# Starting a chunked-attention and feed-forward kernel: units 0 and 1 prepared one after the other, q and k transposed on TensorE, and a new order in block 1

## The chip, the cores and the metric

The kernel runs on one core of a Trainium2 chip. The metric is the device time of one execution in microseconds. Before the change it is 287.82 us, the median of two runs (287.47 and 288.17).

The engines are named as in the profile: PE is the matrix engine (TensorE), with PEld for its loads of weights, DVE is VectorE, ACT is ScalarE, POOL is GpSimd and SP is SyncE. Each engine works through its own instructions in the order in which the program issues them.

## The reference

```python
def _attn_ref(q, k, v):                      # 8 x 8 x 576 x 64
    B, H, S, D = q.shape
    chunk = 64
    ...
    scores = scale * np.matmul(q_c, k_c.transpose(0, 1, 2, 4, 3))
    scores = scores - np.max(scores, axis=-1, keepdims=True)
    attn = np.exp(scores)
    attn = attn / (np.sum(attn, axis=-1, keepdims=True) + 1e-09)
    out = np.matmul(attn, v_c)
    return out.reshape(B, H, S, D).astype(np.float32)

def _moe_ref(x, w_in, w_out, beta):          # 4608 tokens, 512 -> 2048 -> 512
    h = x @ w_in
    g = h * (1.0 / (1.0 + np.exp(-beta * h)))
    return (g @ w_out).astype(np.float32)
```

The attention works inside chunks of 64 tokens of one head. Its output, with the heads side by side, is the input x of the two layers.

## The kernel before

The 4608 tokens are cut into 18 units of 256 tokens, and two units make one of 9 blocks of 512 tokens. For each unit the kernel makes the attention output, normalises it and transposes it, so that the model dimension lies on the partitions (`xt`, one per block). For each block, layer 1 (`emit_m`, L322) makes 16 pieces of 128 hidden features: four products with a slice of `w_in` into a PSUM bank `hps`, a tanh on ACT into `sg` (L339), and (tanh + 1) times h on DVE into `gt` (L343). With beta halved that is twice the gated value, and the 0.5 is put into the copy of the output. Layer 2 (`emit_t`, L354) makes four tiles of 128 tokens, 16 products each, into a bank `ops`; ACT copies it (L371) and SP stores it. Operands are float16, sums float32.

The attention of a unit is: q and k loaded by POOL's queue, which turns float32 into float16; transposed by DVE in blocks of 32 x 32 (`emit_T`, L145); scores (`emit_sc`, L216) as small products that use parts of the PE array side by side; the exponential on ACT (L247) into `et`; products with V (`emit_pv`, L254), in which a column of ones in V's tile gives the sum; a reciprocal and a multiplication on DVE (`emit_norm`, L280). The transpose of the result is either done on PE with a copy by ACT or DVE behind it (`emit_xt_pe`, L298, and `emit_xt_pair`, L306, for a whole unit), or by a transposing DMA of SP for later units.

PSUM has eight banks: four rotate under the tag "p" (`hps`, `ops`, idle products and others), two form the one buffer "s" and two the one buffer "x". A buffer is given out again only when everything that reads it has finished.

The order of all instructions is written out by hand (`tc.manual_schedule()`, L394). From block 3 on a list of due times merges the pieces (L563 to L596); the change touches nothing there.

The start, L395 to L467, handles units 0 and 1 together. SP loads q and k of heads 0 to 3 for both units as float32 (L399 to L404), 512 KB each; POOL loads heads 4 to 7 as float16. Each partition holds four neighbouring tokens, so unit 0 lies on partitions 0 to 63 and unit 1 on 64 to 127. POOL then loads four V tiles, sets `late` between them (L411), builds the identity, and loads the slices of `w_in`, of `w_out` and the next units. PE begins with 78 tiny products and idle products of 512 columns (`emit_idle`, L381), which only keep PE at work; one of them waits for `late` (L425). `emit_T_half(0)` (L174) casts heads 0 to 3 on ACT and transposes them on DVE, `emit_sc_half` (L186) makes scores of four heads of one unit, `emit_ex_half` (L206) their exponential. Then unit 0's products with V, unit 1's scores, normalisation and transposes follow, with idle products between them. Layer 1 begins at L452 with the first four pieces of unit 0's 256 columns (`emit_m(0, m, 0, 256)`), after them come the same four pieces for unit 1's columns (L464), then pieces 4 to 15 for all 512 columns.

Block 1's attention lies in layer 2 of block 0 (L469 to L489): 16 steps of four products, with unit 2's scores at step 8, its products with V at step 10, the transposed pair at step 13, unit 3's scores at step 14 with the exponential in two halves (`split`), and at step 15 the first piece of layer 1 of block 1, unit 3's products with V and its normalisation. The first five pieces of that layer are made for unit 2's columns first (L482 to L494), and the rest for all 512 columns (L495), with the missing halves between them (L498).

The softmax here doesn't subtract the row's maximum and nothing guards it: scores larger than these inputs give would overflow.

## Time and profile before

| What | Value |
|---|---|
| median of the two runs | 287.82 us |
| the profiled execution, its own time | 287.57 us |
| its span, from first to last instruction | 285.8 us |
| instructions | 6671 |
| first product of layer 1 | 15.16 us |
| first product of its second column half | 17.59 us |
| DVE busy, ACT busy, share of the span | 50%, 51% |
| bytes moved by DMA | 37.40 MB |

All times in the profile count from the start of the span. The profiled execution takes 1.8 us longer than its span. The profile gives, for each engine, the time in which it was busy and what ended the time in which it was not; the chain that ended last is followed back from the last instruction, and its share by engine says which engine sets the time. An engine that waits outside that chain costs nothing.

### The profile page before, as it was taken

Reading aid. Unit: us, or ns where it says so; the run is one execution under the profiler, and the core shown is the slowest. Engines: PE = TensorE matmul, PEld = TensorE weight load, DVE = VectorE, ACT = ScalarE, POOL = GpSimd, SP = SyncE. Lnnn points to the kernel's source line nnn. Section 1 sums busy time; section 2 is a strip of 40 time slices with the busy share of each in tenths; the row PEclk is TensorE's granted clock in tenths of the full one; section 3 lists DMA queues with packets and bytes.
Section 4 is the critical chain, followed back from the end, with each engine's and each line's share of the span. In section 5 each row is a group of like instructions: output and inputs, shape, how many; then the busy total and the mean of one; then the engine's idle time right before and its main releaser. Section 6 shows DMA issues by size and latency. Waiting matters only on the chain.

```text
span 285.8 us, 6671 instructions
## 1 busy us (share of the span) xinstructions
PE 279.2 (98%) x2779; PEld 136.5 (48%) x2779; DVE 143.6 (50%) x268; ACT 146.2 (51%) x223; POOL 95.6 (33%) x125
## 2 busy tenths in 40 slices
PE   6989999999999999999999999999999999999995
PEld 3564456544544444444444444444444444444444
DVE  2678444776558553535454536363635463333301
ACT  4478228773557545455554555554546444444411
POOL 8853678488073991168607000000000000000000
PEclk9999999999999999999999999999999999999999
DMA  8999999999999999999999983425311221010012
GB/s 198 177 197 206 182 179 213 209 164 150 207 104 173 178 176 162 170 190 187 168 170 164 174 130 78 100 57 119 79 54 39 73 57 55 37 39 37 37 73 76
DMA packets 141085, 37.40 MB, mean 131 GB/s; under 512 B 128000, under 2 KB 136576, under 8 KB 141056
## 3 DMA queue, kind: packets, MB, share of 16 engines
q0 software_dynamic: 99136, 17.83, 82.3%
q1 hardware_dynamic: 41776, 19.09, 32.5%
q8 instruction: 22, 0.36, 0.5%
q10 hardware_dynamic: 144, 0.07, 0.1%
q14 instruction: 7, 0.06, 0.0%
HBM read 36.71 MB, written 9.44 MB: 161 GB/s over the span
## 4 chain that ended last, share of the span: by engine, by line
PE 96%; POOL 1%; ACT 1%; issue 1%; DVE 0%; DVEq 0%; POOLq 0%
PE hps L329 44%; PE ops L361 43%; PE warm L381 2%; PE x L266 2%; PE sc L238 1%; PE ops L602 1%; PE sc L225 1%; PE y L266 1%; ACT xt L304 1%; POOL h L401 1%; PE sc L198 1%; POOL vbig L113 1%; PE xp L303 0%; ACT et L208 0%; PE xp L311 0%
## 5 line engine op out<-in xcount | busy, mean ns | idle before, releaser
L343 DVE SCALAR_TENSOR_TENSOR gt<-sg,hps 128x512 f16<-128x512 f32 (+1 forms) x153 | 99.2, 655 | 101.9 <-ACT sg L339 101.3
L329 PE MATMUL hps<-xt,win 128*128 128x512 f16 (+1 forms) x612 | 136.2, 367 | 0.8 <-ACT xt L304 0.7
L339 ACT ACTIVATE sg<-hps,beta 128x512 f32<-128x512 f32 (+1 forms) x153 | 100.4, 662 | 71.3 <-PE hps L329 69.7
L361 PE MATMUL ops<-wout,gt 128*128 128x512 f16 x560 | 131.1, 379 | 0.0
L329 PEld LDWEIGHTS <-win 128*128 128x128 f16 x612 | 58.3, 98 | 62.4 <-issue 1.0
L361 PEld LDWEIGHTS <-gt 128*128 128x128 f16 x560 | 54.1, 98 | 64.0
L371 ACT ACTIVATE osb<-ops 128x512 f32<-128x512 f32 x35 | 20.9, 598 | 42.8 <-PE ops L361 42.8
L113 POOL DMA_DIRECT2D vbig<-in_v_dram x40 | 34.0, 867 | 11.9 <-DMA wout<-in_moe_w_out_dram 3.6
L99 POOL DMA_DIRECT2D qu<-in_q_dram x22 | 18.7, 859 | 24.9 <-DMA qT<-qu 22.5
L287 DVE TENSOR_TENSOR x<-x,rd 128x512 f16<-128x512 f32 x27 | 18.7, 691 | 1.0
L99 POOL DMA_DIRECT2D ku<-in_k_dram x22 | 18.7, 874 | 0.9 <-DMA ku<-in_k_dram 0.9
L285 DVE RECIPROCAL rd<-x 128x8 f32<-128x8 f32 x27 | 5.4, 199 | 13.1 <-PE x L266 13.1
L247 ACT ACTIVATE et<-sc 128x1024 f16<-128x1024 f32 (+1 forms) x8 | 6.4, 811 | 8.7 <-PE sc L238 8.7
L231 ACT ACTIVATE et<-sc 128x1024 f16<-128x1024 f32 x10 | 10.2, 1021 | 0.7
L266 PEld LDWEIGHTS <-et 64*64 64x64 f16 x576 | 6.0, 107 | 7.4 <-issue 4.7
L381 PE MATMUL warm<-idle 128*128 128x512 f16 (+1 forms) x32 | 8.0, 401 | 0.0
L287 DVE TENSOR_TENSOR x<-y,rd 128x256 f16<-128x256 f32 x18 | 7.6, 424 | 0.6
L105 POOL DMA_DIRECT2D ku<-in_k_dram x9 | 6.8, 755 | 2.6 <-DMA win<-in_moe_w_in_dram 1.3
L105 POOL DMA_DIRECT2D qu<-in_q_dram x9 | 6.8, 766 | 1.5 <-DMA win<-in_moe_w_in_dram 0.7
L266 PE MATMUL x<-vbig,et 64*64 64x65 f16 x432 | 6.7, 194 | 0.2 <-ACT et L208 0.2
L614 DVE TENSOR_SCALAR osb<-ops 128x256 f32<-128x256 f32 (+1 forms) x2 | 0.7, 358 | 12.1 <-PE ops L602 12.1
L131 POOL DMA_DIRECT2D win<-in_moe_w_in_dram x8 | 6.0, 767 | 1.4 <-DMA vbig<-in_v_dram 1.4
(46 smaller groups left out, 75.3 us busy)
## 6 DMA issues: line engine op xcount, KB each, us to landing
out_dram<-osb SPq DMA_DIRECT2D x35, 256.0 KB, 3.6
vbig<-in_v_dram POOLq DMA_DIRECT2D x32, 128.0 KB, 7.8
qu<-in_q_dram POOLq DMA_DIRECT2D x20, 128.0 KB, 5.7
ku<-in_k_dram POOLq DMA_DIRECT2D x20, 128.0 KB, 7.4
win<-in_moe_w_in_dram POOLq DMA_DIRECT2D x8, 256.0 KB, 8.9
wout<-in_moe_w_out_dram POOLq DMA_DIRECT2D x4, 512.0 KB, 12.2
qu<-in_q_dram POOLq DMA_DIRECT2D x3, 256.0 KB, 7.4
ku<-in_k_dram POOLq DMA_DIRECT2D x3, 256.0 KB, 7.9
```

Of the source, the lines that this page charges most:

```text
L99: nc.gpsimd.dma_start(out=tv[off:off + n, sp], in_=src[b, :, s:s + n, :].rearrange("h p d -> p h d"),)
L105: nc.gpsimd.dma_start(out=t[off // 2:(off + n) // 2], in_=src[b, :, s:s + n, :].rearrange("h (p r) d -> p h r d", r=2),)
L113: nc.gpsimd.dma_start(out=vbig[off:off + n, i, :, 0:D], in_=v[b, :, s:s + n, :].rearrange("h p d -> p h d"),)
L231: nc.scalar.activation(out=et, in_=sc, func=ACTF.Exp, scale=scale)
L266: nc.tensor.matmul(out=(x[0][64 * c:64 * c + 64, r, g, 0:D + 1] if len(x) == 1 else x[r][64 * c:64 * c + 64, g, 0:D + 1]), lhsT=(et[64 * r ...
L287: nc.vector.tensor_tensor(out=o, in0=z[..., 0:D], in1=rd[:, r].to_broadcast(list(o.shape)), op=ALU.mult)
L329: nc.tensor.matmul(out=hps[:, 0:n], lhsT=w_in16[m // 2][:, kk, (m % 2) * 128:(m % 2) * 128 + 128], rhs=xr[:, c0 // CH:(c0 + n) // CH, 2 * ...
L339: nc.scalar.activation(out=sg[:, 0:n], in_=hps[:, 0:n], func=ACTF.Tanh, scale=beta2[:, m:m + 1])
L343: nc.vector.scalar_tensor_tensor(out=gt_t[j][:, m, c0:c0 + n], in0=sg[:, 0:n], scalar=1.0, in1=hps[:, 0:n], op0=ALU.add, op1=ALU.mult,)
L361: nc.tensor.matmul(out=ops, lhsT=gt_t[j][:, kk, t * 128:(t + 1) * 128], rhs=w_out16[kk // 4][:, kk % 4, :], start=(kk == 0), stop=(kk == K ...
L371: nc.scalar.activation(out=osb, in_=ops, func=ACTF.Copy, scale=0.5)
L381: nc.tensor.matmul(out=d[:, 0:w], lhsT=idle[:, 0:128], rhs=idle[:, 0:w])
```

## The change

At the start, units 0 and 1 are handled apart. The float32 loads on SP and on ACT's queue now bring q and k of unit 0 for all heads, heads 0 to 3 on partitions 0 to 63 and heads 4 to 7 on partitions 64 to 127, 256 KB per load; POOL loads those of unit 1 in the same layout, in four loads, behind the identity and two V tiles and ahead of the first slice of `w_in`. Instead of DVE's transposes, PE transposes q and k with the identity into PSUM, and ACT and DVE copy them into `qkT0`: for unit 0 in 16 transposes of 128 columns, for unit 1 in 32 of 64 columns. The casts of unit 0 are shared between ACT and DVE. The scores of a unit are then 32 products over 64 rows in place of 64 over 32 rows with two summands. Layer 1 begins with two pieces of unit 0 between unit 1's scores and its products with V. The tile `late` and the wait for it go; a tile `spare` is there for one early exponential and for eight small copies after block 0's layer 1.

In block 1, unit 2's scores, its products with V and its transposed pair stand at steps 10, 12 and 14 of layer 2; unit 3's scores come after the last step, with one exponential for all of them, then three pieces of layer 1, then unit 3's products with V. Seven pieces instead of five are made for unit 2's columns first.

```diff
-    late = const.tile([128, 16], FP16)
+    spare = const.tile([128, 1], FP16)
...
-    qkT0 = [[const.tile([128, HH, 128, 2], FP16, name=f"t0{i}{a}") for i in range(2)] for a in range(2)]
+    qkT0 = [[const.tile([128, 2, 2, 64, 4], FP16, name=f"t0{i}{u}") for i in range(2)] for u in range(2)]
...
-    def emit_T_half(a):
-        for i, h0, h1 in ((0, 0, HH), (1, 0, HH // 2), (1, HH // 2, HH)) if a == 0 else ((0, 0, HH), (1, 0, HH)):
-            src = qk0[a][i][:, h0:h1]
-            if a == 0:
-                nc.scalar.copy(out=src, in_=raw0[i][:, h0:h1])
...
-    def emit_sc_half(u, a):
...
+    tq_t = {}
+
+    def emit_cast_first(i, hp, cast):
+        hs = slice(2 * hp, 2 * hp + 2)
+        to = qk0[0][i].rearrange("p h r d -> p (h r d)").rearrange("p (r h d) -> p h r d", r=4, h=HH)
+        cast(out=to[:, hs], in_=raw0[i][:, hs])
+
+    def emit_T_first(u, i, hp):
+        if (u, i) not in tq_t:
+            tq_t[u, i] = ps_p.tile([128, 2, 4, 128], FP16, tag="p", name="tq")
+        z = qk0[u][i].rearrange("p h r d -> p (h r d)")
+        for r in range(4):
+            if u == 0:
+                nc.tensor.transpose(
+                    out=tq_t[u, i][:, hp, r, :],
+                    in_=z[:, (r * HH + 2 * hp) * D:(r * HH + 2 * hp + 2) * D], identity=ident)
+                continue
+            for hh in range(2):
+                o = ((2 * hp + hh) * 4 + r) * D
+                nc.tensor.transpose(
+                    out=tq_t[u, i][64 * hh:64 * hh + 64, hp, r, :], in_=z[:, o:o + D], identity=ident)
+
+    def emit_cp_first(u, i, hp, copy):
+        hp = hp if isinstance(hp, slice) else slice(hp, hp + 1)
+        copy(
+            out=qkT0[u][i][:, hp].rearrange("p g a i r -> p g (a i) r"),
+            in_=tq_t[u, i][:, hp].rearrange("p g r x -> p g x r"),
+        )
+
+    def emit_sc_first(u):
+        et_t[u] = et_p.tile([128, 2, H, CH], FP16, tag="et", name="et")
+        sc = x_t["sc", u] = ps_s.tile([128, 2, H, CH], FP32, tag="s", name="sc")
+        qt, kt = (z.rearrange("p g a i r -> p g a (i r)") for z in qkT0[u])
+        for s in range(2):
+            for a in range(2):
+                for hp in range(2):
+                    for par in range(2):
+                        for c in range(2):
+                            t0 = 128 * s + 64 * c
+                            nc.tensor.matmul(
+                                out=sc[64 * c:64 * c + 64, par, 4 * s + 2 * a + hp, :],
+                                lhsT=kt[64 * par:64 * par + 64, hp, a, t0:t0 + 64],
+                                rhs=qt[64 * par:64 * par + 64, hp, a, t0:t0 + 64],
+                            )
+
+    def emit_ex_first(u, s):
+        js = slice(4 * s, 4 * s + 4)
...
-    def emit_pv(u, where=("x", "s")):
-        et = et_t.pop(u)
-        for s in (1, 0) if u >= MU else (0, 1):
+    def emit_pv(u, where=("x", "s"), which=None):
+        et = et_t[u]
+        for s in which or ((1, 0) if u >= MU else (0, 1)):
...
-                            lhsT=(et[64 * r:64 * r + 64, s, 4 * c + g, :] if u < XU else
+                            lhsT=(et[64 * r:64 * r + 64, s, 4 * c + g, :] if 2 <= u < XU else
...
-    def emit_xt_pe(u, s, copy=nc.scalar.copy):
+    def emit_xt_pe(u, s, copy=nc.scalar.copy, tag=None):
...
-        tag = "s" if u < 2 and (u, s) != (1, 0) else "xp"[s]
+        tag = tag or "xs"[s]
...
-        for a, eng, dst in ((0, nc.sync, raw0), (1, nc.gpsimd, qk0[1])):
+        def load_first(u, engs, dst):
             for i, src in enumerate((q, k)):
-                eng.dma_start(
-                    out=dst[i],
-                    in_=src[0, HH * a:HH * a + HH, 0:2 * UNIT, :].rearrange("h (p r) d -> p h r d", r=4),
-                )
+                for a in range(2):
+                    engs[a].dma_start(
+                        out=dst[i][64 * a:64 * a + 64],
+                        in_=src[0, HH * a:HH * a + HH, u * UNIT:(u + 1) * UNIT, :].rearrange(
+                            "h (p r) d -> p h r d", r=4),
+                    )
+
+        load_first(0, (nc.sync, nc.scalar), raw0)
+        nc.scalar.activation(out=spare, in_=tiny[:, 0:1], func=ACTF.Exp)
+        make_identity(nc, ident)
         bv = moe_beta.rearrange("(m w f) -> w m f", w=4, f=32)
         for w in range(4):
             nc.sync.dma_start(out=braw[32 * w:32 * w + KFF, :], in_=bv[w])
-        for i in range(4):
-            load_v(i)
-            if i == 1:
-                nc.gpsimd.memset(late, 0.0)
+        load_v(0)
+        load_v(1)
+        load_first(1, (nc.gpsimd, nc.gpsimd), qk0[1])
+        load_w_in(0)
+        load_v(2)
+        load_v(3)
         nxt[0] = 2
-        make_identity(nc, ident)
-        for g in range(8):
+        for g in range(1, 8):
             load_w_in(g)
         for g in range(3):
             load_w_out(g)
@@ -419,83 +439,96 @@
         load_w_out(3)
...
-        emit_tiny(78)
+        emit_tiny(85)
         warm = idle_bank()
+        emit_idle(7, 512, warm)
+        act_cp, vec_cp = nc.scalar.copy, nc.vector.tensor_copy
+        for i in range(2):
+            emit_cast_first(i, 0, act_cp)
+            emit_cast_first(i, 1, vec_cp)
+            emit_T_first(0, i, 0)
+            emit_cp_first(0, i, 0, act_cp)
+            emit_T_first(0, i, 1)
+            emit_cp_first(0, i, 1, vec_cp)
+            emit_idle((3, 1)[i], 512, warm)
+        nc.vector.transpose(out=bt, in_=braw)
+        emit_sc_first(0)
+        emit_ex_first(0, 0)
+        emit_ex_first(0, 1)
         emit_idle(3, 512, warm)
-        nc.tensor.matmul(out=warm[:, 0:16], lhsT=idle[:, 0:128], rhs=late)
-        emit_idle(8, 512, warm)
-        emit_T_half(0)
-        emit_sc_half(0, 0)
-        emit_ex_half(0, 0)
+        emit_pv(0, "xs", (0,))
+        emit_norm(0, 0)
+        emit_idle(2, 512, warm)
+        emit_pv(0, "xs", (1,))
+        emit_norm(0, 1)
+        emit_T_first(1, 0, 0)
+        emit_T_first(1, 0, 1)
+        emit_cp_first(1, 0, slice(0, 2), act_cp)
         warm = idle_bank()
-        emit_idle(6, 512, warm)
-        emit_T_half(1)
-        nc.vector.transpose(out=bt, in_=braw)
-        emit_sc_half(0, 1)
-        emit_ex_half(0, 1)
-        emit_sc_half(1, 0)
+        emit_xt_pe(0, 0, tag="x")
+        emit_T_first(1, 1, 0)
+        emit_T_first(1, 1, 1)
+        emit_cp_first(1, 1, 0, act_cp)
         emit_idle(2, 512, warm)
+        emit_xt_pe(0, 1, vec_cp, tag="x")
+        emit_cp_first(1, 1, 1, vec_cp)
+        emit_idle(1, 512, warm)
+        emit_sc_first(1)
+        emit_ex_first(1, 0)
+        emit_ex_first(1, 1)
         loads_to(5)
-        emit_pv(0, ("s", "p"))
-        emit_sc_half(1, 1)
-        emit_ex_half(1, 0, 2)
-        emit_norm(0, 0)
-        emit_norm(0, 1)
+        nc.scalar.activation(out=beta2, in_=bt[:, 0:KFF], func=ACTF.Copy, scale=0.5)
+        d = [emit_m(0, m, 0, 256, True) for m in (0, 1)]
+        emit_pv(1, "xs", (0,))
+        emit_norm(1, 0)
         emit_idle(1, 512, warm)
-        emit_idle(12, 64, warm)
-        emit_xt_pe(0, 0)
-        emit_pv(1, ("x", "p"))
+        emit_idle(13, 64, warm)
+        emit_pv(1, "xs", (1,))
         emit_norm(1, 1)
-        emit_norm(1, 0)
-        nc.scalar.activation(out=beta2, in_=bt[:, 0:KFF], func=ACTF.Copy, scale=0.5)
-        emit_xt_pe(0, 1)
-        d = [emit_m(0, m, 0, 256, True) for m in (0, 1)]
         d[0][0]()
-        emit_xt_pe(1, 1)
+        d.append(emit_m(0, 2, 0, 256, True))
+        emit_xt_pe(1, 0, tag="x")
         d[1][0]()
-        d.append(emit_m(0, 2, 0, 256, True))
-        d[0][1]()
-        emit_xt_pe(1, 0, nc.vector.tensor_copy)
         d.append(emit_m(0, 3, 0, 256, True))
-        for act, _ in d[2:]:
-            act()
-        for _, vec in d[1:]:
+        emit_xt_pe(1, 1, tag="s")
+        d[2][0]()
+        d[3][0]()
+        for _, vec in d:
             vec()
         for m in range(4):
             emit_m(0, m, 256, 256)
         for m in range(4, KFF):
             emit_m(0, m)
         emit_T(2)
+        for _ in range(8):
+            nc.scalar.activation(out=spare, in_=tiny[:, 0:1], func=ACTF.Copy)
         for i in range(16):
-            if i == 8:
+            if i == 10:
                 emit_sc(2)
-            if i == 10:
+            if i == 12:
                 emit_pv(2)
                 emit_norm(2, 0)
                 emit_norm(2, 1)
                 emit_T(3)
-            if i == 13:
+            if i == 14:
                 emit_xt_pair(2)
-            if i == 14:
-                emit_sc(3, True)
-            if i == 15:
-                a0, v0 = emit_m(1, 0, 0, 256, True)
-                a0()
-                emit_pv(3)
-                emit_norm(3, 0)
-                emit_norm(3, 1)
-                v0()
-                emit_m(1, 1, 0, 256)
             emit_t(0, i % 4, 4 * (i // 4), 4 * (i // 4) + 4)
-        emit_xt_pe(3, 0)
-        emit_m(1, 2, 0, 256)
-        emit_xt_pe(3, 1)
+        emit_sc(3)
+        for m in range(3):
+            emit_m(1, m, 0, 256)
+        emit_pv(3)
+        emit_norm(3, 0)
+        emit_norm(3, 1)
         emit_m(1, 3, 0, 256)
         emit_m(1, 4, 0, 256)
-        for m in range(5, KFF):
+        emit_xt_pe(3, 0)
+        emit_m(1, 5, 0, 256)
+        emit_xt_pe(3, 1)
+        emit_m(1, 6, 0, 256)
+        for m in range(7, KFF):
             emit_m(1, m)
-            if m < 10:
-                emit_m(1, m - 5, 256, 256)
+            if m < 14:
```

The lines that the diff cuts out of `emit_T_half`, `emit_sc_half` and `emit_ex_half` are removed as a whole; `emit_ex_first(u, s)` is the exponential of four of the eight columns of heads of one unit. With `tag` not given, `emit_xt_pe` takes the buffer "x" for a unit's first tile and "s" for the second; before, it took "x" and a bank of "p" for units above 1. That touches units 3 and 5, whose calls stand at L490, L492, L525 and L526; unit 6's scores follow at L527.

## The prediction, made before the result was known

> **What bounds the kernel now.** I read the page first, then the waits of PE, then the busy time by stretches, then the chain of work that ended last at the start, and last the order of time around block 1 and unit 5.
>
> ```profile
> PE 279.2 (98%) x2779; PEld 136.5 (48%) x2779; DVE 143.6 (50%) x268; ACT 146.2 (51%) x223; POOL 95.6 (33%) x125
> ...
> PE 96%; POOL 1%; ACT 1%; issue 1%; DVE 0%; DVEq 0%; POOLq 0%
> ```
>
> PE (TensorE) is busy 98% of the span and is 96% of the chain. Where the other 2% lie, the stretches show (span, then busy time of PE, PEld, DVE, ACT, POOL):
>
> ```profile
> 0.00:17.60 17.60, 14.42 (x336) 8.39 (x336) 9.56 (x25) 8.48 (x14) 13.31 (x23) 1.00 1.40 189
> 17.60:50.00 32.40, 32.31 (x359) 17.21 (x360) 18.19 (x35) 18.48 (x33) 20.66 (x27) 1.00 1.65 195
> 50.00:120.00 70.00, 70.00 (x822) 33.98 (x821) 42.94 (x78) 40.12 (x62) 39.14 (x48) 1.00 1.97 171
> ```
>
> From 17.6 to 50 us PE idles 0.09 us, from 50 to 268 none. So whatever the change does is read at two points: when PE's unbroken stream begins, and whether anything that is changed behind that breaks it. The chain at the start (start us, us, what):
>
> ```profile
> 4.99 3.43 PE warm L381 x8
> ...
> 14.52 0.59 ACT xt L304
> ...
> 15.16 1.03 PE hps L329 x8
> ...
> 17.11 0.43 DVE xt L304
> ...
> 17.59 2.57 PE hps L329 x19
> ```
>
> Layer 1 begins at 15.16; its second column half (columns 256 to 511, unit 1) begins at 17.59, and there is no wait after that. 17.59 is the mark I compare with. Eight idle 512-column products take 3.43 us here (0.43 each, half pace), the later ones 0.216: PE came to full pace near 9.1, 4.3 us after it resumed at 4.82.
>
> Prices that I reuse, from the groups by form (0 to 50 us; xcount, then busy us and mean ns):
>
> ```profile
> L208 ACT ACTIVATE et<-sc 128x512 f16<-128x512 f32 x2 | 1.2, 597 | 3.1 <-PE sc L198 3.1
> L314 ACT COPY xt<-xp 128x1024 f16<-128x1024 f16 x1 | 1.0, 1007 | 0.0
> L304 DVE COPY xt<-xp 128x512 f16<-128x512 f16 x1 | 0.4, 423 | 0.3 <-PE xp L303 0.3
> ```
>
> Others: ACT cast 128x512 0.61, ACT copy 128x512 0.58, DVE normalisation 0.21 + 0.69 (0.93 with the step between), tanh of 256 columns 0.48, its DVE product 0.42, four transposes 0.40, 16 products with V 0.32. One engine follows another after about 0.05.
>
> **The change, part by part: loads.** SP and ACT now issue q and k of unit 0, all heads, 256 KB each; the bytes are those of before (512 KB of q landing at 0.74 + 3.9 = 4.65, of k at 1.27 + 4.9 = 6.16), so I keep 4.65 and 6.16. Bounds: 0.5 earlier, if two queues fill the engines sooner (they moved 208 GB/s between 2 and 3 us, 375 after), 0.5 later, if the queues disturb each other. ACT's two issues (0.46 each, as SP's) and its table load (1.28) end near 3.3, hidden by the landing. On POOL the memset of `late` (0.17) goes, the identity (0.28 + 0.29) comes first, v0 and v1 move ahead of unit 1's q and k, which become four issues (0.6 to 0.9 each) instead of two. Their loads landed at 7.24 and 8.62; two V loads ahead of them (1024 packets each, about 1100 a us by the DMA view of 8 to 11 us, so 0.9 each) make it about 9.0 and 10.4. w_in's first slice moves ahead of v2 and v3 (14.26 to about 12.5); the second stays at 15.6. SP's beta loads stay behind its two issues, as before.
>
> **Unit 0.** The removed wait for `late` (1.24 us of PE) leaves PE at work from 0.96; with 4.3 us as before it is at full pace near 5.3. The 85 tiny products (0.015 each) and 7 idles (0.43) end at 5.2, before the casts do. The DVE transposes of q and k (1.07, 0.64, 0.64) go. Instead, for q: casts on ACT and DVE side by side 4.65 to 5.26 (DVE's cast is not in the trace; bounds 0.42 and 0.69, taken as ACT's 0.61), 4 + 4 transposes 5.31 to 6.1, copies on ACT to 6.53 and on DVE to 6.57. DVE's copy gathers 4 elements from far apart; its bounds are 0.42 (L304, same source and size) and 1.07 (L179, the strided DVE transpose), and I take 0.42, the nearer row. For k: casts to 7.18, transposes to 7.82, ACT copy to 8.23, DVE copy to 8.29. Scores begin at 8.3, where the first half of before began at 8.35: no gain, but now for all eight heads. Exponentials 8.6 to 9.2 and to 9.8; V products at 9.3 and, behind two idles, 9.9; normalisations to 10.63 and 11.57 (before: 12.97 and 14.06).
>
> **Unit 1, behind it.** 16 transposes of q from 10.05 (q landed about 9.0) end at 11.1: by four in 0.40 and 0.055 for each more; halved, if 64-column pairs run beside each other. ACT then does in order: both copies of q 11.15 to 12.16 (1.01), x of tile 0 to 12.74, half of k to 13.32. The transposes of x tile 1 share bank pair "x" with tile 0, so they wait for ACT until 12.8; DVE copies x to 13.67 and the other half of k to 14.1. Only then can unit 1's scores start (14.15), and behind them layer 1 (14.5, against 15.16). Queued behind that wait on PE are layer 1's first products, though unit 0's x is ready at 13.67. Then exponentials 14.5 to 15.1 and 15.7, V products at 15.4 and, after 14 idles (0.75), at 16.3, normalisation of tile 1 to 17.6, transposes to 18.05; ACT, with a tanh (to 16.4), a copy (to 17.93) and a tanh (to 18.4) ahead of it, copies the last x to 19.0. The second column half begins at 19.05 instead of 17.59: **+1.5 us**. The four first halves are done by then in both, so this is all loss. Bounds: 0.5 earlier landing and 0.5 on each transposing half give about 0; a DVE copy of 1.07 delays q, k and unit 1's k, together about 2, and gives +3.4.
>
> **Block 1.** Eight one-element ACT instructions (0.22 each, as the beta scale) run after block 0's tanh, where ACT idled 6.9 us: nothing; if that cover were gone, 1.8. Unit 2's scores two steps later cost nothing: its transposes ended at 35.9, 0.8 us before the scores, so there is more slack. Two more split halves (m = 5, 6) have the same columns: nothing. The order for unit 3 does cost. In before, DVE goes from the V products straight to the normalisations, and multiplies the gates afterwards (start, us):
>
> ```profile
> 45.99 0.21 DVE L285 RECIPROCAL rd<-x 128x8 f32<-128x8 f32 x1 [3.27 <-PE x L266]
> 46.23 0.69 DVE L287 TENSOR_TENSOR x<-x,rd 128x512 f16<-128x512 f32 x1
> ...
> 47.68 0.74 DVE L343 SCALAR_TENSOR_TENSOR gt<-sg,hps 128x256 f16<-128x256 f32 x2
> ```
>
> In the new order three gate products stand ahead of unit 3's normalisations on DVE, and they need three tanh that stand on ACT behind the undivided exponential (1.02). From the start of the scores: they end at 0.7, exponential to 1.8, tanh to 2.3, 2.75, 3.25, third gate product to 3.7, first normalisation to 4.65. PE has until its transposes 0.6 + 3 x 0.43 + 0.38 + 2 x 0.43 = 3.15 of work: it waits 1.5. Then one m (0.43), 0.3 until the second normalisation, and 0.5 until ACT has copied x before m = 7: **+2.3 us**. In before PE had 0.87 twice more to do there, layer 2's last two tiles. Bounds: 1.0 if ACT starts the exponential half a us earlier and its copies overlap, 2.8 if DVE and ACT lag more.
>
> **Unit 5's transposes.** `emit_xt_pe` now takes the banks "s" where it took one of "p" for a unit's second tile. Unit 3's is harmless, unit 5's isn't: unit 6's scores come right behind it on PE and need "s". In before:
>
> ```profile
> 72.25 0.61 PE L303 MATMUL xp<-ident,x 128*128 128x128 f16 x8
> 72.67 1.07 ACT L304 COPY xt<-xp 128x512 f16<-128x512 f16 x2 [1.83 <-PE xp L303]
> 72.79 0.60 PEld L238 LDWEIGHTS <-kT 32*64 32x64 f16 x64
> ```
>
> The scores start at 72.79, while ACT copies until 73.74. With one bank for both they wait for that: PE idles **+1.0 us** (0.8 if the copies run closer, 1.1 at most by the two copies' 1.07).
>
> Sum against the profiled execution (span 285.8, its own time 287.57; the median 287.82 is 0.25 above): 287.57 + 1.5 + 2.3 + 1.0 = 292.4. Measurement tells about 2% from no change, 5.8 us, so this is inside it.
>
> A rule against the change. The trace's 16 transposes between 13.0 and 17.1, in 4.1 us with other products, left PE at 0.216 for 512 columns. The Trainium skill ("TensorE: Matmul & The Clock Gate", Part 4: PE-mode transpose) says that transposes don't count as PE activity for the clock gate in the way products do. This case's row speaks against a fall, but with fewer transposes than the 48 that are added. By the row the sum is 292.4; by the rule, with a spell at half pace in the start, about 295.
>
> **The rivals.** B, block 1's wait is covered: the normalisations aren't late, since ACT comes sooner to the exponential. For it: ACT was only 51% busy; against it: the fixed order on ACT and DVE. 287.57 + 1.5 + 1.0 = 290.1, between 288.6 and 291.
>
> C, not slower: unit 0 alone starts the stream early enough to pay for block 1 and unit 5. Place: ACT's queue between 11.1 and 14.1, in which unit 1's copies stand before unit 0's x. For it: x of unit 0 is normalised 2.5 us sooner. It decides from a second half at 14.3 or earlier, 3.3 gained, which would need unit 1's chain 4.75 shorter than I read; 287.5 or under, down to 285.
>
> D, slower by over 2%: the clock falls to half pace between 9 and 15, while transposes and short idles are all that PE does. For it: half pace held until 9.1 in before, after a pause of 1.24 us; against it: the 16 transposes above. A spell of 4.3 us of work at half pace loses 2.1 to 3.5; it decides from 1.2 lost: 294.5 to 295.9, say 295.2.
>
> Given back later, the +4.8 can't be: from 17.6 to 268 PE idles only 0.09 in before.
>
> **How the numbers follow.** Forecast 0.60 (own range 290.3 to 294.3: the ends of the start come seldom with those of block 1), B 0.16, C 0.07, D 0.14, anything else 0.03. The range 287.2 to 295.2 leaves out most of C, half of D and the rest, about 0.15. Slower by over 2% (above 293.6): D and the top of the forecast's range, 0.14 + 0.11 = 0.25. Faster by over 2% (under 282.1): 0.02, beyond C's end. Within: 0.73.
>
> **What would show it.** In the changed profile: scores of unit 0 near 8.3; unit 1's near 14.2, waiting for DVE's last copy; the first layer 1 product near 14.5; PE idle about 1 us before the second column half at 19; in block 1 the transposes of x of unit 3 waiting about 1.5 us for DVE, with three gate products ahead of the normalisation; unit 6's scores waiting 1 us for ACT's copy; 0.216 per 512 columns all the while. It is wrong if the second half starts before 17.6, if PE doesn't idle in block 1, or if idles after 10 us show 0.43.

## The result, and the profile after

The changed kernel took 297.75 us (median of 2 runs, 297.51 to 297.99) against 287.82 (287.47 to 288.17): 9.9 us slower, a ratio of 1.0345 with an interval of 1.028 to 1.041. The prediction was 292.4 with a range to 295.2, so the time lies 2.6 us above the range. The profiled execution took 297.99 with a span of 296.2 (before 287.57 and 285.8): the span grew by 10.4. Line numbers of the code are now those of the changed kernel.

The page of the changed kernel: busy time of the engines, the granted TensorE clock in 40 slices of 7.4 us, and the chain of work that ended last, by engine.

```profile
PE 282.7 (95%) x2778; PEld 138.8 (47%) x2778; DVE 142.1 (48%) x266; ACT 150.0 (51%) x237; POOL 96.7 (33%) x126
...
PEclk9689999999999999999999999999999999999999
...
PE 91%; DMA 3%; ACT 2%; DVE 1%; issue 0%; SPq 0%; DVEq 0%; ACTq 0%
```

PE works 3.5 us more than before, of which 3.3 are the 48 transposes that DVE did before (2.0 at L187, 1.3 at L193), and idles some 7 us more (13.5 of 296.2 instead of 6.6 of 285.8). In the chain a DMA has 3%, where before had none, and the second clock slice shows 6. Both point to the start. The stretches (span, then busy time of PE, PEld, DVE, ACT and POOL, granted clock, DMA share, GB/s):

```profile
0.00:17.60 17.60, 11.04 (x194) 5.52 (x195) 4.03 (x12) 4.99 (x8) 12.34 (x22) 0.81 1.29 153
17.60:60.00 42.40, 39.63 (x505) 22.31 (x501) 22.98 (x46) 26.38 (x52) 25.94 (x35) 1.00 1.64 196
60.00:100.00 40.00, 39.06 (x563) 20.24 (x562) 25.21 (x49) 22.77 (x38) 18.48 (x22) 1.00 1.49 129
```

Up to 17.6 us PE was busy for 11.04 us, before 14.42; ACT for 4.99 of 8.48; DVE for 4.03 of 9.56, of which 4.08 were the transposes it no longer does. From 60 to 100 PE idles 0.94, from 100 to 280 not at all; what it idles after that, 3.2, it idled at the end before, too (3.3). The chain at the start (start us, us, what):

```profile
1.54 9.22 DMA raw<-in_k_dram
...
10.84 0.63 ACT h L179
...
14.23 0.59 PE sc L213 x17
14.82 1.40 PE warm L394 x3
...
20.96 0.41 PE sc L213 x28
...
25.85 1.25 PE hps L342 x10
```

The 256 KB of unit 0's k that SP issues (heads 0 to 3) take 9.22 us to land, at 10.76; I had kept 6.16. The second half of unit 0's scores, predicted for 8.3, begins at 14.23, unit 1's at 20.96, and the second column half at 25.85: +8.26 against 17.59. Three idle products take 1.40 at 14.82: half pace. PE's waits (total us, times, longest):

```profile
PE tq L187 <- ACT h L179: 4.0, 2, 2.8
PE tq L187 <- ACT t L198: 1.3, 2, 0.7
```

The first line is PE waiting for the casts, that is for q and k to land; 2.8 us of it is k's. The second was in no step of mine: the second four transposes of q, and of k, wait 0.67 until ACT has copied the first four.

In block 1 (start us, us; the brackets are idle time before, and what ended it), first ACT's and DVE's order, then PE's (unit 3's scores begin on PE at 53.54):

```profile
54.31 1.02 ACT L260 ACTIVATE et<-sc 128x1024 f16<-128x1024 f32 x1
55.23 1.20 ACT L352 ACTIVATE sg<-hps,beta 128x256 f32<-128x256 f32 x3
...
55.73 1.15 DVE L356 SCALAR_TENSOR_TENSOR gt<-sg,hps 128x256 f16<-128x256 f32 x3 [3.22 <-ACT sg L352]
56.80 0.20 DVE L298 RECIPROCAL rd<-x 128x8 f32<-128x8 f32 x1
```

```profile
57.78 0.40 PE L316 MATMUL xp<-ident,x 128*128 128x128 f16 x4 [0.77 <-DVE x L300]
...
59.71 2.54 PE L342 MATMUL hps<-xt,win 128*128 128x512 f16 x14 [0.25 <-ACT xt L317]
```

Three gate products stand ahead of unit 3's normalisation, as predicted, and PE waits for it: 0.77 and then 0.25, 1.02 in sum instead of 2.3. Unit 6's scores wait for ACT's copy of unit 5's x, as predicted (1.0):

```profile
83.32 0.70 PE L251 MATMUL sc<-qT,kT 32*64 32x64 f16 x64 [0.94 <-ACT xt L317]
```

Start 8.26, block 1 1.02, unit 5 0.94: 10.2 of the 10.4 by which the span grew. So the question for the runs is the start: why does k land 4.6 us late, and what does the rest of the 8.26 consist of?

### The profile page after: what moved, and what is told of

Its sections match the earlier page's. It is cut to its first block, busy times and chain, and to the rows that moved or that the text cites. A ratio compares the mean times of both kernels' runs of the same rounds, so it can differ in the third digit from the quotient of the medians.

```text
span 296.2 us, 6692 instructions
## 1 busy us (share of the span) xinstructions
PE 282.7 (95%) x2778; PEld 138.8 (47%) x2778; DVE 142.1 (48%) x266; ACT 150.0 (51%) x237; POOL 96.7 (33%) x126
## 4 chain that ended last, share of the span: by engine, by line
PE 91%; DMA 3%; ACT 2%; DVE 1%; issue 0%; SPq 0%; DVEq 0%; ACTq 0%
PE hps L342 42%; PE ops L374 41%; DMA raw<-in_k_dram 3%; PE x L279 2%; PE sc L251 1%; PE ops L635 1%; PE sc L238 1%; ACT xt L317 1%; PE warm L394 1%; PE y L279 1%; ACT t L198 1%; DVE t L198 0%; PE xp L316 0%; ACT sg L352 0%; PE tq L187 0%
## 5 line engine op out<-in xcount | busy, mean ns | idle before, releaser
L342 PEld LDWEIGHTS <-win 128*128 128x128 f16 x620 | 58.9, 98 | 61.7 <-issue 1.4
L300 DVE TENSOR_TENSOR x<-x,rd 128x512 f16<-128x512 f32 x29 | 20.0, 691 | 1.1
L244 ACT ACTIVATE et<-sc 128x1024 f16<-128x1024 f32 x10 | 10.2, 1022 | 0.7
L279 PE MATMUL x<-vbig,et 64*64 64x65 f16 x464 | 7.4, 195 | 0.0
L187 PE MATMUL tq<-ident,h 128*128 128x128 f16 x16 | 2.0, 262 | 5.4 <-ACT h L179 4.0
L300 DVE TENSOR_TENSOR x<-y,rd 128x256 f16<-128x256 f32 x14 | 5.9, 424 | 0.5
```

Source lines behind the costliest of these rows:

```text
L244: nc.scalar.activation(out=et, in_=sc, func=ACTF.Exp, scale=scale)
L279: nc.tensor.matmul(out=(x[0][64 * c:64 * c + 64, r, g, 0:D + 1] if len(x) == 1 else x[r][64 * c:64 * c + 64, g, 0:D + 1]), lhsT=(et[64 * r ...
L300: nc.vector.tensor_tensor(out=o, in0=z[..., 0:D], in1=rd[:, r].to_broadcast(list(o.shape)), op=ALU.mult)
L342: nc.tensor.matmul(out=hps[:, 0:n], lhsT=w_in16[m // 2][:, kk, (m % 2) * 128:(m % 2) * 128 + 128], rhs=xr[:, c0 // CH:(c0 + n) // CH, 2 * ...
```

## The experiments

Theories on the loads: (a) the two queues of SP and ACT disturb each other; (b) POOL's loads, which run from about 5 us on, take the DMA engines from them; (c) the cutting does it, since every load now reaches 64 of the 128 partitions; (d) cutting into smaller transfers as such. Beside these, the price of the half pace, of the two PSUM waits, and of block 1 and unit 5 each by itself. The times of before were measured again beside each run (medians 287.61 to 287.96).

**All four loads on SP** (changed kernel).

```
-load_first(0, (nc.sync, nc.scalar), raw0)
+load_first(0, (nc.sync, nc.sync), raw0)
```

> The changed kernel with all four loads of unit 0's q and k issued by SP, none by ACT. Theory two queues (the halves disturb each other because they stand in two queues): q lands near 4.7 and k near 6.2 as before the change, the second column half starts some 4.5 us earlier, near 21, and the time falls from 297.8 to about 293. Theory halves (a load of 64 partitions is slow wherever it is issued): k stays at 9.5 or later and the time above 296. Theory POOL (the tail of k shares the DMA engines with POOL's loads): k stays near 10, as POOL's loads are unchanged.

Measured: 299.19 (298.57 to 299.62), ratio 1.039 (1.037 to 1.042). q landed near 7.0, k at 11.4, both later than with two queues. Part of that is the order of issue: SP starts the last load of k at 2.83 instead of 1.54. But from there it still takes 8.53 us, far from the 4.9 of before. One queue doesn't bring the time back, so (a) falls.

**POOL's loads held until k has landed** (changed kernel): an element of k is copied on POOL ahead of its first load.

```
+nc.gpsimd.tensor_copy(out=gate, in_=raw0[1][:, 0, 0, 0:1])
 load_v(0)
 load_v(1)
```

> The changed kernel, with a one-element POOL copy of k ahead of POOL's first load, so that POOL's loads start only when unit 0's k has landed. Theory POOL: k lands near 6.5 instead of 10.8, unit 0's scores start near 9 instead of 13.7; unit 1's q and k come some 3 us later than they would, near 13, and the time is 293 to 295. Theories two queues and halves: k lands at 8.5 or later although nothing else is loaded, and the time is 297 or more, as POOL's loads are later for nothing.

Measured: 300.09 (299.26 to 302.61), ratio 1.044 (1.039 to 1.049). ACT's cast of k, its first instruction that needs k:

```profile
8.95 0.62 ACT L179 CAST h<-raw 128x512 f16<-128x512 f32 x1 [1.13 <-DMA raw<-in_k_dram]
```

It starts at 8.95 instead of 10.84, so POOL's loads cost k 1.9 us. With nothing else loading, k still lands 2.7 later than in before (8.87 against 6.16). (b) is a part, not the cause. What the queues moved, from 0 to 7 us and from 7 to 8:

```profile
DMA packets 1129, 1.05 MB, mean 150 GB/s; under 512 B 126, under 2 KB 1128, under 8 KB 1128
...
DMA packets 71, 0.02 MB, mean 18 GB/s; under 512 B 57, under 2 KB 71, under 8 KB 71
```

All but the last pieces of the four loads (1.05 MB in all) have moved by 7 us. The last 15 pieces of 1 KB of SP's k follow one after another, from 7.34 to 8.39, and only then does k land. In before the last 15 pieces took 0.2 us, until 5.59. So of the 2.7 about 2.0 is the slower bulk, and 0.8 is this tail. The changed kernel has it too (its last 15 pieces take 1.3, until 9.58); no run here shows where it comes from.

The time is no better, since unit 1 now is late (PE waits 0.53 and 0.47 for its q and k) and this execution ran at half pace until about 20 us.

**16 idle products instead of 3 while PE waits for k** (changed kernel), to hold the clock.

```
-emit_idle((3, 1)[i], 512, warm)
+emit_idle((16, 1)[i], 512, warm)
```

> The changed kernel with 16 instead of 3 idle products behind q's transposes, so that PE works while it waits for k. Theory clock: PE stays at full pace (granted clock 1.0 from 10 to 16 us in place of 0.5), the stretch from k's landing to unit 1's transposes gets 1.5 to 2 us shorter, and the time falls to about 296. If the half pace is hidden under ACT's and DVE's copies: under 0.7 us gained, 297.1 or more.

Measured: 297.91 (296.85 to 299.34), ratio 1.035 (1.031 to 1.040). The granted clock stayed at 1.00, but the first seven of these idles still ran at half pace (0.43 each, until 11.4), and all of them until 13.4, 3 us past k's landing; the second half began at 26.43. Inconclusive: too many of them.

**The cutting alone, by partitions** (kernel before; each of its two loads, 128 partitions of 4 heads, becomes two of 64 partitions).

```
+for hf, e2 in enumerate((nc.sync, nc.scalar)):
+    e2.dma_start(
+        out=dst[i][64 * hf:64 * hf + 64],
+        in_=src[0, 0:HH, hf * UNIT:(hf + 1) * UNIT, :].rearrange("h (p r) d -> p h r d", r=4))
```

> The kernel before, with only its two float32 loads each cut into two of 64 partitions, the first issued by SP, the second by ACT, and POOL's loads unchanged. Theories two queues and halves: k lands near 10 in place of 6.2, and the time rises by 3 us or more, to 291 or above. Theory POOL: POOL's first loads are the same and start as early, so k lands late as well, if the raw loads are not done when POOL's begin. If k still lands near 6.2, the cause is POOL's new order, with the V tiles first, and the time stays at 287.8.

Measured: 292.18 (291.74 to 293.33), ratio 1.016 (1.013 to 1.019): the loads alone cost 4.2 us. k is cast at 9.64 instead of 6.16, 3.5 later, and layer 1 begins at 19.25 instead of 15.16, 4.1 later:

```profile
9.64 1.14 ACT L178 CAST h<-raw 128x512 f16<-128x512 f32 x2 [1.31 <-DMA raw<-in_k_dram]
...
11.75 2.60 PE L381 MATMUL warm<-idle 128*128 128x512 f16 x6
```

ACT's table load (1.28) runs here only behind q's landing, at 5.98, but ACT then stands idle for 1.31 until k has landed, so it isn't on the path. Of the other 0.6 a part is half pace: the six idle products ahead of the second scores take 2.60, in before 1.64.

**The same cutting by heads**: two loads of 256 KB again, on the same two queues, with the same 1 KB pieces, but each over 128 partitions (kernel before).

```
+for hf, e2 in enumerate((nc.sync, nc.scalar)):
+    e2.dma_start(
+        out=dst[i][:, 2 * hf:2 * hf + 2],
+        in_=src[0, 2 * hf:2 * hf + 2, 0:2 * UNIT, :].rearrange("h (p r) d -> p h r d", r=4))
```

> The kernel before, with its two float32 loads each cut into two of 256 KB on SP and ACT as in the last experiment, but by heads, so that each load still reaches all 128 partitions. Theory partitions (a load that reaches 64 partitions moves at about half the rate): k lands by 6.6 and the time stays within 0.5 us of 287.9. Theory cutting (twice as many loads, on two queues, are slow as such): k lands at 8.5 or later and the time is 291 or more, as when they were cut by partitions.

Measured: 288.12 (287.96 to 289.92), ratio 1.0029 (1.001 to 1.0048). (d) costs 0.5 us by the medians (0.3 to 1.4 by the interval) where the cut by partitions costs 4.2, so (c) holds. Even of the 0.5 a part may be ACT's table load, which here, too, runs only behind q's landing (1.28 from 4.63) and is in the chain. The stretch from 4 to 5 us, in which these loads have the DMA engines nearly to themselves (span, busy time of DVE, granted clock, mean DMA share, GB/s), for before, the changed kernel, the one with POOL held, and this one:

```profile
4.00:5.00 1.00, 0.00 (x0) 1.00 1.08 374
```

```profile
4.00:5.00 1.00, 0.00 (x0) 1.00 1.15 220
```

```profile
4.00:5.00 1.00, 0.00 (x0) 1.00 1.16 223
```

```profile
4.00:5.00 1.00, 0.00 (x0) 1.00 1.06 363
```

Read the last two numbers together: the DMA engines are fully occupied in all four (share 1.06 to 1.16), but with 64-partition loads they move 220 GB/s instead of 370, so the same bytes keep them busy 1.8 times as long. In the stretch before, from 3 to 4 us, the gap is smaller: 276 (the changed kernel) and 292 (POOL held) against 375 (before) and 345 (this one). The issues and their landings (KB, us to landing) say the same, first the changed kernel, then this one:

```profile
raw<-in_k_dram SPq DMA_DIRECT2D x1, 256.0 KB, 9.2
```

```profile
raw<-in_k_dram SPq DMA_DIRECT2D x1, 256.0 KB, 4.7
```

The Trainium skill states the rule ("SBUF — State Buffer", Door 1: The DMA port swizzle): partitions 0 to 63 reach only 8 of the 16 ports and 64 to 127 the other 8, so such a load has half the rate, about 218 GB/s of 436, and ("Can I just issue two DMAs to hit both halves?") two loads at partitions 0 and 64 together gained only 6%. The 220 GB/s with two such loads in flight agree with it; the 276 to 292 of the us before are above it. It is a rule that speaks against this change, and the prediction didn't weigh it.

**The changed kernel with the loads of before** (both on 128 partitions, and POOL's too). The values then lie in the wrong heads, so only its time is read.

```
-load_first(0, (nc.sync, nc.scalar), raw0)
+for i, src in enumerate((q, k)):
+    nc.sync.dma_start(out=raw0[i],
+        in_=src[0, 0:HH, 0:2 * UNIT, :].rearrange("h (p r) d -> p h r d", r=4))
```

> The changed kernel with the loads of q and k as they were before, in four DMAs of 128 partitions in place of eight of 64, POOL's order as changed; the data in the tiles are then not those that the rest of the start expects, so only the time is read. Theory partitions: k lands near 6.3, unit 0's scores start near 8.8, the second column half near 19.6 to 20.2 in place of 25.85, PE stays at full pace, and the time is 291.5 to 292.5. If the landing was only a part and the half pace of the clock comes from the transposes: the granted clock is 0.5 for some us between 8 and 16 all the same, and the time is 294 or more.

Measured: 294.31 (292.67 to 295.49), ratio 1.0225 (1.019 to 1.026); the profiled execution took 292.67. Its loads moved 370 GB/s from 4 to 5 us, q was there by 4.68 and k by 6.27. The median lies where I had expected a half pace from the transposes (294 or more); the profiled execution, the fastest of the four, shows none. Parts of its chain at the start:

```profile
9.65 0.41 PE sc L213 x28
...
15.54 0.41 PE sc L213 x28
...
20.43 6.66 PE hps L342 x38
```

The second half begins at 20.43: +2.84, where I had +1.5. From unit 0's second scores on my sum holds: 5.89 to unit 1's (I had 5.85), 4.89 from there to the second half (4.90). The first agreement is partly luck: DVE's copy of unit 1's k adds 0.61 where I had 0.42, and the steps ahead of it are 0.14 shorter. All 1.35 lie ahead of 9.65 (I had 8.3). They are 0.67 for the second transposes of q, which wait for ACT's copy, twice 0.27 for DVE's gathering copies (0.69 instead of 0.42, L198), and 0.14 for DVE's cast of k (0.75 instead of 0.61); smaller differences cancel. The scores of 28 products take 0.41 and the transposes 0.40 for four: full pace, with all 48 transposes, in this execution.

**The same with a tile, and so a PSUM bank, of its own for each half of unit 0's transposes** (and a fresh bank for the idle products behind q's).

```
-if (u, i) not in tq_t:
+if u == 0:
+    tq_t[u, i, hp] = ps_p.tile([128, 4, 128], FP16, tag="p", name="tq")
+elif (u, i) not in tq_t:
     tq_t[u, i] = ps_p.tile([128, 2, 4, 128], FP16, tag="p", name="tq")
...
-                    out=tq_t[u, i][:, hp, r, :],
+                    out=tq_t[u, i, hp][:, r, :],
```

> The changed kernel with the loads of before (as in the sixth experiment, data not in the place that the start expects, so only its time is read), and in addition unit 0's two transposed halves of q, and of k, each in a PSUM bank of its own. Theory bank: PE's wait of 0.7 us for ACT's copy, between the two halves, goes; unit 0's scores end near 9.2 in place of 10.0, the second column half begins near 19.7 in place of 20.4, and the time is 0.5 to 1 us under the sixth experiment's. If the wait only moves to the next copy on DVE: no earlier than 20.2, and the same time.

Measured: 291.88 (291.85 to 291.91), ratio 1.0135 (1.011 to 1.016). In its chain:

```profile
8.82 0.41 PE sc L216 x28
...
19.59 7.52 PE hps L345 x42
```

PE's wait for ACT's copy is gone, and everything behind it comes 0.84 earlier. So the wait came from the sharing: PE didn't write one half while ACT was to read the other. The halves here got a tile and a bank of their own at once, so the runs don't tell whether the program's order for one tile or the bank asks for it. Between the medians of this run and the one before the gain is larger, 2.4; see the next but one.

**9 idle products instead of 3** (changed kernel), as many as fit the wait.

```
-emit_idle((3, 1)[i], 512, warm)
+emit_idle((9, 1)[i], 512, warm)
```

> The changed kernel with 9 in place of 3 idle products behind q's transposes, so that PE works until about when k lands, and not past it. Theory clock: the granted clock is 1.0 from 10 to 16 us in place of 0.5, unit 0's V products begin 1 us earlier after k's landing, and the time is 0.7 to 1.5 us under the changed kernel's, near 296.7. If half pace was hidden under the copies: 297.2 or more.

Measured: 297.06 (296.78 to 298.26), ratio 1.0323 (1.029 to 1.035). From 10 to 15 us the clock is granted in full now (0.50 in the changed kernel):

```profile
10.00:15.00 5.00, 3.84 (x50) 1.81 (x48) 1.23 (x3) 1.60 (x3) 3.68 (x5) 1.00 1.76 180
```

k is cast at 10.7 (10.84 in the changed kernel), layer 1 begins at 20.36 instead of 21.31. So filling the wait gave back 0.95 us in the trace; the medians differ by 0.7, but the runs overlap (296.78 to 298.26 against 297.51 and 297.99), so the times alone don't show it. The nine idles also outlast the wait: k's transposes begin 1.1 behind its cast's start instead of 0.7.

**The start alone**, with the loads, block 1 and banks of before (values misplaced as above).

```
+for i, src in enumerate((q, k)):
+    nc.sync.dma_start(out=raw0[i],
+        in_=src[0, 0:HH, 0:2 * UNIT, :].rearrange("h (p r) d -> p h r d", r=4))
...
-emit_sc(3)
-for m in range(3):
-    emit_m(1, m, 0, 256)
...
+if i == 14:
+    emit_sc(3, True)
...
-tag = tag or "xs"[s]
+tag = tag or "xp"[s]
```

> The changed kernel's start alone: with the loads of before (data not in the place that the start expects, so only its time is read), and block 1's order and the banks of the later transposes as before. If the parts add up, it is the sixth experiment's time less 1.7 and 1.1 us, 290.8 to 291.8, and its profile has the second column half near 20.4 and no wait of PE behind it. If the later waits had hidden one another: 292.5 or more.

Measured: 293.7 (291.97 to 294.93), ratio 1.019 (1.016 to 1.023). A miss: by its time it falls to the other theory, that the later waits hide one another, but its profile shows another reason. The start is instruction by instruction that of the run with the old loads, and still the profiled execution (294.93) has its second half at 23.9 instead of 20.43. Its timeline on PE, and its stretch from 10 to 15:

```profile
11.57 1.46 PE L394 MATMUL warm<-idle 128*128 128x512 f16 x3
...
13.33 1.04 PE L394 MATMUL warm<-idle 128*128 128x512 f16 x2
```

```profile
10.00:15.00 5.00, 4.77 (x80) 1.99 (x80) 1.92 (x5) 1.08 (x2) 3.10 (x5) 1.00 1.78 182
```

Three idle products take 1.46 (0.82 in the run with the old loads, at 9.99): half pace until about 17 us, though PE is busy for 4.77 of 5 us and the granted clock reads 1.00. With this start full pace, read from the durations of idles and transposes, was there by 5.5 us in two profiled executions (old loads, own banks), by 6.7 (the change), 7.7 (all on SP), 11.4 (9 and 16 idles), 17 (this one) and 20 (POOL held); in before and in four kernels with its start (cut by heads, block 1 alone, the bank alone, fewer idles), by 7.4 to 9.7. Between the run with the old loads and this one the second half differs by 3.5 us. That would also explain the spread of 2.8 us between the runs with the old loads; it is argued, since each kernel has one trace. The four runs with own banks lie within 0.06 of each other, and there the first eight transposes follow without a gap. What sets the moment, the gaps or the transposes, wasn't separated. Nor is the fastest run here, 291.97, explained: it is 1.3 above what the profiled execution with the old loads leaves without PE's waits in block 1 and unit 5 (292.67 less 1.02 and 0.94).

**Block 1 alone** (kernel before with the new order of block 1 and the eight small ACT instructions).

```
-if i == 14:
-    emit_sc(3, True)
...
+emit_sc(3)
+for m in range(3):
+    emit_m(1, m, 0, 256)
+emit_pv(3)
+emit_norm(3, 0)
+emit_norm(3, 1)
...
```

> The kernel before with the new order of block 1 alone (with the eight small ACT copies, without the changed banks). The prediction's term was +2.3; the profile of the changed kernel shows PE idle 0.77 + 0.25 us there, so +1.0, 288.9. If the waits were absorbed behind, 287.9.

Measured: 289.58 (288.76 to 289.77), ratio 1.0059 (1.0040 to 1.0079): +1.7 us (1.15 to 2.3). PE's waits in its profile have the predicted one, 0.8, and 0.3 for an output store; the rest, about 0.6, I can't place.

```profile
PE xp L304 <- DVE x L288: 0.8, 1, 0.8
PE hps L330 <- DMA out_dram<-osb: 0.3, 1, 0.3
```

**Bank "s" for unit 5 alone** (kernel before).

```
-tag = "s" if u < 2 and (u, s) != (1, 0) else "xp"[s]
+tag = "s" if u < 2 and (u, s) != (1, 0) else ("xs" if u == 5 else "xp")[s]
```

> The kernel before with the banks 's' for the transposes of unit 5's second tile alone. The prediction's term was +1.0, and the profile of the changed kernel shows PE waiting 0.9 us for ACT's copy: 288.8. If it is given back later: 287.9.

Measured: 288.81 (288.29 to 289.27), ratio 1.0038 (1.0025 to 1.0051): +1.1 us, with one wait of 0.9 of the scores for ACT's copy in the profile.

**The kernel before with 3 idle products instead of 6** ahead of its second transposes.

```
-emit_idle(6, 512, warm)
+emit_idle(3, 512, warm)
```

> The kernel before with 3 in place of 6 idle products ahead of its second set of scores. Their transposes end at 9.8 us, the idle products at 10.55, so the stream could begin up to 0.65 us earlier: 287.0. If the idle products were what brought PE to full pace: half pace lasts a us or more longer and the time is the same or higher.

Measured: 287.51 (287.11 to 288.41), ratio 0.9981 (0.9967 to 0.9995): some 0.5 us faster than before (0.1 to 1.0), the only one of these kernels that is. In its chain:

```profile
2.12 6.92 DMA h<-in_k_dram
...
10.01 0.18 DVE bt L433
...
17.44 9.69 PE hps L329 x52
```

With the idles out of the way the landing of POOL's k (9.05) and, behind it, a DVE transposition of beta are what the second scores wait for; the second half comes at 17.44 instead of 17.59.

## Why the prediction was wrong, point by point

**The loads: the failed step.** The step is "the bytes are those of before [...], so I keep 4.65 and 6.16", with bounds of 0.5 either way. The bytes were the same, the partitions of each load weren't. From 4 to 5 us loads of 64 partitions moved 220 GB/s, those of 128 about 370, these on one queue or two. q came at 5.94 and k at 10.76: +4.6. Of that, 2.7 is there with no other load beside it (8.87 with POOL held): about 2.0 from the slower bulk, 0.8 from the tail of SP's k, whose cause stays open. The other 1.9 follows: a load that isn't done by 5 us meets POOL's loads, which before came behind it. My bounds were those of a theory of queues alone and left out the shape of the loads. The lower rate accounts for the bulk: the 1.05 MB of q and k take 2.8 us at 374 GB/s and 4.8 at 220, 2.0 more. That rate stood in no row of before; the rule above would have given it as a half.

**Unit 0.** Scores predicted for 8.3 came at 14.23: 4.6 from the loads, 0.67 from the shared bank, 0.4 from two groups of four transposes at half pace (0.61 instead of 0.40), 0.27 from DVE's gathering copy. Smaller terms cancel: DVE, which my working kept busy until 6.57, was free for k's cast (0.4 less), and short gaps add up to as much. The copy's bounds (0.42 and 1.07) held and the value taken was wrong: 0.69. The bank wait wasn't in the sum at all. The step "4 + 4 transposes 5.31 to 6.1, copies on ACT to 6.53" let PE run on while ACT copied; with both halves in one tile of one bank that didn't happen.

**Unit 1 and the second half.** From unit 0's scores on, my working held to 0.05 at full pace, in part because two errors cancel (old loads: 5.89 and 4.89 for 5.85 and 4.90). In the changed kernel 0.84 is added by the half pace (6.73 for 5.89). So the term "+1.5" measured +8.26: 4.6 loads, 1.34 in the three other steps ahead of the scores (0.67, 0.4 and 0.27), 0.84 half pace behind them; these add to 6.8, as 8.26 less 1.5 does.

**Block 1.** The mechanism was right: three gate products ahead of the normalisation, PE waiting for the x of unit 3, then for its copy. Its size was 1.02 in the trace for a predicted 2.3: at the low bound, but not for the reason that the bound named. ACT didn't come to the exponential sooner: the exponential ended 1.79 after the scores' start, as in my working (1.8). The three tanh behind it took 1.20, not 1.45, and the normalisation was done 4.2 after that start instead of 4.65. PE had 3.5 of work ahead of the transposes instead of 3.15, so it waited 0.77 instead of 1.5. Behind them it waited 0.25 instead of 0.8. By itself, in the runs, block 1 cost 1.7, with an interval (1.15 to 2.3) that just reaches my term; the trace decides here. PE has no wait at the eight small ACT instructions, at unit 2's scores or at the two more split halves. Rival B, no wait at all, didn't happen.

**Unit 5.** Right: 1.0 predicted, 0.94 in the trace, +1.1 in the runs.

**Rival C**, that unit 0 alone begins early enough to pay, didn't happen: even with the old loads unit 1's scores, not unit 0's, set layer 1 (15.54), and the start stays 2.84 later, 2.0 with own banks.

**Rival D**, the clock. Idles after 10 us showed 0.43 and more each, which I had named as the sign. In the changed kernel's trace the fall has a plain cause, and not the one I gave: PE waits 2.8 us for k, and the granted clock is 0.50 after it. On the path it cost about 1.2 us (0.4 ahead of unit 0's scores and 0.84 behind them), not 2.1 to 3.5; 9 idles gave back 0.95 of it, net of their own overrun. The rule on transposes that the prediction weighed ("TensorE: Matmul & The Clock Gate", Part 4) isn't needed for it: in the profiled executions with the old loads and with own banks, the same 48 transposes ran at full pace throughout. But the executions in which full pace came only at 11.4, 17 and 20 us are not explained, and no run here took the transposes away from them; there the rule may bear.

**The sum.** Predicted 292.4, profiled 297.99, 5.6 apart: start +6.8, block 1 -1.3, unit 5 -0.1, which leaves 0.2. Without the loads' cutting the changed kernel takes 292.67 to 295.49, so even then the forecast would have stood just under the lowest run. No part of the change was found to gain: the start (with the old loads), block 1 and the bank each cost time by themselves.

## What to carry to other kernels

When a load is re-cut, ask first which partitions each piece reaches, and price it by GB/s over these partitions; equal bytes on two queues are not equal time. A transfer that ends later also ends among others: look at what starts when it should be over (POOL's loads at 5 us here, 1.9 us). When a producer's tile is cut so that the consumer may start on the first half, give the halves tiles and banks of their own; here the producer stopped for the consumer's read until they had them.

## What the runs showed of the hardware that was not expected

- From 4 to 5 us 64-partition loads on two queues moved 220 GB/s with the DMA engines fully occupied, 128-partition ones of the same pieces 363 to 374, on two queues or one.
- A load was late by its last pieces: with POOL held, 1.05 MB had moved by 7.0 us, and the last 15 KB took from 7.34 to 8.39.
- The time at which PE reaches full pace varied from 5.5 to 20 us between executions with nearly the same instructions on PE, and the granted clock reads 1.00 in this first slow spell (three 512-column products in 1.46 at 11.57). It shows 0.50 only for a fall that comes later. The duration of an idle product is the safer sign: 0.216 or 0.43.
- PE's four transposes into one half of a bank waited 0.67 us for ACT's copy out of the other half; with a tile and a bank for each the wait was gone.
- Copies of 128x512 fp16 out of PSUM that gather four elements from 256 bytes apart took ACT 0.59 (as a plain copy) and DVE 0.69 (plain 0.42).
- A load of 256 KB over 64 partitions took SP 0.74 and 0.86 us to issue (0.60 to 0.73 with all four on SP), one of 256 KB or 512 KB over 128 partitions 0.45 to 0.48.
